# Cross-covariance attention with a mixture of adapters: transposes in 32-bit words of two bf16 channels, and gating weights with A in one operand

## The chip, the cores and the metric

The kernel runs on one core of a Trainium2 chip. The time is device microseconds of one execution. Three runs of the kernel before gave a median of 253.76 us (253.75 to 253.85).

## The reference

There are four batches of N = 6400 rows and C = 256 channels, in float32. Each batch goes through cross-covariance attention, and its result through a mixture of eight adapters of rank 16, of which each row uses two:

```python
qn = q / (np.linalg.norm(q, axis=1, keepdims=True) + 1e-06)
kn = k / (np.linalg.norm(k, axis=1, keepdims=True) + 1e-06)
s = kn.transpose(0, 2, 1) @ qn / tau          # 256 x 256 per batch
a = softmax(s, axis=-1)
x = v @ a                                      # 25600 rows in all
logits = x @ w_gate                            # 8 experts, the best two per row
w = softmax(logits of the best two)
out = x + sum over the two: w * ((x @ A[e]) @ B[e])
```

(`softmax` stands here for the lines of the reference that subtract the maximum, exponentiate and divide.)

## The kernel before, in words

**Layout.** A chunk is 128 rows of one batch, 50 chunks to a batch, 25 pairs of chunks. Partition p of a batch holds 50 neighbouring rows, so that a load of n chunks moves a stretch of n rows into each partition. q, k and v are cast to bf16 by their loads, which GpSimd issues (L212); all but the first piece of q, which SyncE loads as float32. One core does everything.

**First half of a batch: the 256 x 256 matrix.** `gram` (L344) multiplies, for each chunk and each half `ic` of the channels, 128 channels of k (stationary) with all 256 channels of q (moving) into one accumulator `acc` (L350). Beside it the squares of q and k are taken (L323, L326), pairs of chunks added (L335), and summed over the rows by a product with ones (`norm`, L365). `chain0` to `chain6` then make the softmax: roots and reciprocals of the norms, scaling, a product of `ones_f` with a diagonal matrix in float32 (L404) that spreads q's norms over the partitions, and the exponential `ae` (L415).

**From the softmax to the operands of the second half.** `chain4` (L420) transposes `ae` into `aT`: four 128 x 128 transposes of bf16 (L428), whose stationary operand takes every second column, and one copy out of PSUM (L432). `chain5` (L438) multiplies `aT` with `wg_sb`, the gating weights (8 columns, L445), and with `A_sb` (all adapters' A, 128 columns, L447), eight products for a batch, and scales the result into `wa_sb`. `chain6` makes `a_bf`, the softmax itself in bf16.

**Second half: rows of v.** A unit is two pairs, four chunks (or one pair at the end of a group).
- `transposes` (L498): eight 128 x 128 transposes of v in bf16 (L511), then one copy out of PSUM into `vT` on ScalarE or VectorE (L518, L521). `vT` holds `[half of the channels, chunk, row]`.
- `logits` (L530): 8-column products of `vT` with the first 8 columns of `wa_sb` (L539), for a whole group of units; `gating` (L546) makes the two weights of each row from them on VectorE, by a handful of small operations.
- `z_gz` (L634): 128-column products of `vT` with the rest of `wa_sb` (L643), and one VectorE product with the gates (L647) into `gz`, `[chunk, expert and rank]`.
- `gz_t` (L654): a transpose of `gz` for each chunk (L659), and a copy into `gzT` (L664, L667).
- `y_mm` (L671) and `delta` (L681): for each chunk two 256-column products of `vT` with `a_bf` (L676) and one of `gzT` with `ball_sb`, all adapters' B (L685), into one PSUM tile; a copy to `ys` (L695, L698).
- `send` (L708): stores of up to ten pairs, issued by GpSimd for most of the run, by ScalarE and SyncE near the end. The last two, of four pairs and of one, go out through SyncE (L731).

**What sets the order.** There is no scheduler at run time. The main loop (L760) plays through a model of the engines, with a clock for each (`run("pe", 0.1125 * nch)` is the cost that it books for a unit's transposes), and writes each engine's instructions in the order that comes out. The same model picks ScalarE or VectorE for a copy (`quicker`, L527) and the moment at which a load is issued (`load_more`, L179: at most six tiles of q and k and three of v are held). TensorE gets the chain of the next batch first, then logits, then the pairs' stages or the next batch's `gram`, whichever is behind.

Of the kernel before, what the change touches and what calls it, by code (L numbers as in the profile page):

```python
# [8 lines left out]
FP32 = mybir.dt.float32  # L9
BF16 = mybir.dt.bfloat16  # L10
# [6 lines left out]
def kernel(  # L17
# [47 lines left out]
    STAGED = []  # L65
# [159 lines left out]
    for lo, hi in zip([0] + STAGED, STAGED + [P]):  # L225
        nc.sync.dma_start(stage[lo:hi], q_v[0, lo:hi, 0:FIRST, :])
# [32 lines left out]
    wg_sb = const.tile([P, CC, E], BF16)  # L259
    A_sb = const.tile([P, CC, ER], BF16)  # L260
# [9 lines left out]
    def constants():  # L270
        V = nc.vector
        V.tensor_copy(wg_sb.rearrange("p cc e -> p (cc e)"), wst)
# [6 lines left out]
        V.tensor_copy(shift[:, E:E + P].rearrange("p (g j) -> p g j", j=E)[:, :, 0], grp)  # L279
        for e in range(E):  # L280
            V.tensor_scalar(out=a_wide[:, :, e, :], in0=ast, scalar1=own[:, e:e + 1],
                            scalar2=None, op0=OP.mult)

    def constant_a():
        full = ps_t.tile([P, 512], FP32, tag="pt", name="A_ps")
        ap = full.rearrange("p (c k) -> p c k", c=CC)[:, :, 0:ER]
        for j in range(E):
            for cc in range(CC):
                nc.tensor.matmul(
                    ap[:, cc, :], shift[:, E - j:E - j + P],  # L290
                    a_wide[:, CC * j + cc, :, :].rearrange("p e r -> p (e r)"),
                    start=(j == 0 and cc == 0), stop=(j == E - 1), skip_group_check=True)
        nc.vector.tensor_copy(A_sb, ap)
# [126 lines left out]
    def chain4(b):  # L420
        d = st[b]
        ae = d["ae"]
        aT_ps = ps_t.tile([P, 512], FP32, tag="pt", name="aT_ps").bitcast(BF16).rearrange(
            "p (a c i) -> p a c i", a=2, c=CC)[:, 0, :, :]
        aev = ae.rearrange("p ic (m cc) -> p ic cc m", cc=CC)
        for cc in range(CC):
            for ic in range(CC):
                nc.tensor.matmul(aT_ps[:, cc, ic * P:(ic + 1) * P], aev[:, ic, cc, :], ident,  # L428
                                 is_transpose=True, start=(cc == 0 and ic == 0),
                                 stop=(cc == CC - 1 and ic == CC - 1))  # L430
        aT = tmp.tile([P, CC, C], BF16, name="aT")
        nc.vector.tensor_copy(aT, aT_ps)  # L432
        rec = bat.tile([P, CC], FP32, name="rec")
        nc.vector.reciprocal(rec, d["se"])
        d["aT"], d["rec"] = aT, rec
        d["at"] = run("dve", 0.6, run("pe", 0.25, d["at"]))

    def chain5(b):  # L438
# [4 lines left out]
        for ic in range(CC):  # L443
            for cc in range(CC):
                nc.tensor.matmul(wa[:, ic, 0:E], aT[:, cc, ic * P:(ic + 1) * P], wg_sb[:, cc, :],  # L445
                                 start=(cc == 0 and ic == 0), stop=False, skip_group_check=True)
                nc.tensor.matmul(wa[:, ic, E:E + ER], aT[:, cc, ic * P:(ic + 1) * P],  # L447
                                 A_sb[:, cc, :],
                                 start=False, stop=(cc == CC - 1 and ic == CC - 1),
# [48 lines left out]
    def transposes(u):  # L498
# [4 lines left out]
        vT = vt_pool.tile([P, CC, 4, P], BF16, tag="vT", name="vT")[:, :, 0:nch, :]  # L503
        full = ps_t.tile([P, 512], FP32, tag="pt", name="vT_ps")
        pt = full.bitcast(BF16).rearrange("p (c s t) -> p c s t", c=CC, s=4)[:, :, 0:nch, :]
        i = 0
        for sc in range(nch):
            s, o = v_at[2 * p + sc]
            vt = tiles["v"][b, s]
            for ic in range(CC):  # L510
                nc.tensor.matmul(pt[:, ic, sc, :], vt[:, o, ic * P:(ic + 1) * P], ident,  # L511
                                 is_transpose=True, start=(i == 0), stop=(i == 2 * nch - 1))
                i += 1
# [3 lines left out]
        if quicker(0.16 + 0.213 * nch, 0.14 + 0.142 * nch) == "act":  # L517
            nc.scalar.copy(vT, pt)  # L518
# [11 lines left out]
    def logits(gr):  # L530
# [5 lines left out]
        for u in range(gr["u0"], gr["u1"]):  # L536
            for sc in range(2 * units[u]["n"]):
                for ic in range(CC):
                    nc.tensor.matmul(lp[:, i, :], units[u]["vT"][:, ic, sc, :], st[b]["wa"][:, ic, 0:E],  # L539
# [94 lines left out]
    def z_gz(u):  # L634
# [6 lines left out]
        for sc in range(nch):  # L641
            for ic in range(CC):
                nc.tensor.matmul(z[:, sc, :], r["vT"][:, ic, sc, :], st[b]["wa"][:, ic, E:E + ER],  # L643
                                 start=(sc == 0 and ic == 0), stop=(sc == nch - 1 and ic == 1),
                                 skip_group_check=True)
        gz = work.tile([P, 4, ER], BF16, tag="gz", name="gz")[:, 0:nch, :]
        nc.vector.tensor_tensor(  # L647
            out=gz.rearrange("p c (e r) -> p c e r", e=E),
# [5 lines left out]
    def gz_t(u):  # L654
        r = units[u]
        nch = 2 * r["n"]
        gt = r["zg"].bitcast(BF16)[:, 0:512].rearrange("p (s d) -> p s d", s=4)[:, 0:nch, :]
        for sc in range(nch):
            nc.tensor.matmul(gt[:, sc, :], r["gz"][:, sc, :], ident, is_transpose=True,  # L659
                             start=(sc == 0), stop=(sc == nch - 1))  # L660
        gzT = work.tile([P, 4, ER], BF16, tag="gzT", name="gzT")[:, 0:nch, :]
        t_end = run("pe", 0.056 * nch)
        if quicker(0.16 + 0.107 * nch, 0.14 + 0.071 * nch) == "act":
            nc.scalar.copy(gzT, gt)  # L664
            r["gzT_end"] = run("act", 0.16 + 0.107 * nch, t_end)
        else:
            nc.vector.tensor_copy(gzT, gt)  # L667
# [3 lines left out]
    def y_mm(p):  # L671
        r, x = unit_of[p]
        y = ps_y.tile([P, 2, C], FP32, tag="y", name="y_ps")
        for sc in range(2):
            for ic in range(CC):
                nc.tensor.matmul(y[:, sc, :], r["vT"][:, ic, 2 * x + sc, :], st[r["b"]]["a"][:, ic, :],  # L676
# [4 lines left out]
    def delta(p):  # L681
        r, x = unit_of[p]
        gr, y = stores[p], pr[p]["y"]
        for sc in range(2):
            nc.tensor.matmul(y[:, sc, :], r["gzT"][:, 2 * x + sc, :], ball_sb, start=False,  # L685
# [258 lines left out]
```

## Time and profile before

| what | value |
|---|---|
| median of three runs | 253.76 us |
| the profiled execution | 253.88 us |
| its span, from the first to the last instruction | 252.1 us |
| mean granted TensorE clock | 0.945 |
| transposes of v, mean of one (L511) | 219 ns, 400 of them |
| transposes of the gated z, mean of one (L659) | 219 ns, 200 of them |
| copies of vT: VectorE (L521), ScalarE (L518) | 36 of 659 ns, 16 of 1014 ns |
| copies of gzT: VectorE (L667), ScalarE (L664) | 33 of 409 ns, 19 of 577 ns |
| HBM read and written | 78.91 and 26.21 MB |

A group's row in the profile reads: line, engine, operation, output <- input, shape, count | busy us, mean ns of one | idle time of the engine before it, and what ended most of that. PE is TensorE's products, PEld its loads of stationary operands, which run beside the products. Products are pipelined: the mean of one is from its start to its modelled end, and the next one starts long before that, so the spacing of products is read from the chain of waits, where a row gives the start, the length and the count of a run of products. A row of a window gives, after the stretch and its length, the busy us of PE, PEld, DVE, ACT and POOL with their counts, the granted clock, the DMA share and GB/s. Loads that cast to bf16 are counted in GB/s by what they write, which is half of what they read.

### The profile page before, as it was taken

What the parts mean: (1) busy time and instruction counts of PE and PEld (TensorE: products, weight loads), DVE (VectorE), ACT (ScalarE), POOL (GpSimd) and SP (SyncE); (2) the same over time, 40 slices, a digit from 0 to 9 for tenths busy, and PEclk for the clock granted to TensorE, in tenths of its full rate; (3) what the DMA queues carried; (4) which work ended last, traced back from release to release, by engine and by line L of the source; (5) the groups of instructions that cost most, each with busy time, mean ns of one, the idle gap of its engine ahead of it and who ended that gap; (6) DMA issues with size and microseconds to landing.
All of it is one profiled execution on the core that took longest, in us unless ns stands there. A gap on an engine that the chain in (4) does not pass through costs nothing.

```text
span 252.1 us, 6727 instructions
## 1 busy us (share of the span) xinstructions
PE 205.5 (82%) x2870; PEld 183.5 (73%) x2870; DVE 165.2 (66%) x420; ACT 167.1 (66%) x256; POOL 31.1 (12%) x63
## 2 busy tenths in 40 slices
PE   0457087576499999999999899898999989999950
PEld 0344076465478999999989788797998878999940
DVE  1541646784539688887957798769687677687510
ACT  2654065873739779899565698966798757586640
POOL 8111003004001200030401101030020000010000
PEclk9997659999859999999999999999999999999995
DMA  7999999999999999999999999999999999999995
GB/s 218 214 214 212 238 220 213 212 217 213 216 214 218 216 213 215 214 216 215 216 409 230 214 217 216 251 414 388 221 217 218 256 376 305 432 432 408 424 423 217
DMA packets 8902, 66.76 MB, mean 265 GB/s; under 512 B 984, under 2 KB 1128, under 8 KB 5416
## 3 DMA queue, kind: packets, MB, share of 16 engines
q0 software_dynamic: 7872, 60.04, 94.2%
q10 hardware_dynamic: 432, 3.74, 3.5%
q1 hardware_dynamic: 568, 2.56, 2.7%
q8 instruction: 22, 0.36, 0.5%
q14 instruction: 8, 0.07, 0.1%
HBM read 78.91 MB, written 26.21 MB: 417 GB/s over the span
## 4 chain that ended last, share of the span: by engine, by line
DMA 42%; PE 39%; DVE 6%; issue 5%; ACT 3%; POOL 2%; DVEq 0%; POOLq 0%; ACTq 0%
DMA vt<-in_v_dram 14%; PE y_ps L676 10%; DMA kt<-in_k_dram 10%; DMA qt<-in_q_dram 10%; DMA bst<-in_moe_B_dram 8%; PE acc L350 8%; PE y_ps L685 5%; PE zg L643 4%; PE vT_ps L511 4%; PE zg L659 2%; PE lp L539 2%; DVE s L335 2%; ACT sq L326 2%; PE nrm L365 1%; ACT ys L698 1%
## 5 line engine op out<-in xcount | busy, mean ns | idle before, releaser
L698 ACT COPY ys<-y_ps 128x512 f32<-128x512 f32 x92 | 52.1, 586 | 15.6 <-PE y_ps L685 14.3
L350 PE MATMUL acc<-qt,kt 128*128 128x256 bf16 x400 | 56.7, 293 | 5.4 <-DMA kt<-in_k_dram 5.4
L676 PE MATMUL y_ps<-a_bf,vT 128*128 128x256 bf16 x400 | 59.2, 272 | 1.6 <-ACT ys L698 1.5
L326 ACT ACTIVATE sq<-qt 128x1024 bf16<-128x1024 bf16 (+1 forms) x42 | 40.7, 1013 | 14.6 <-DVE s L335 11.0
L326 ACT ACTIVATE sq<-kt 128x1024 bf16<-128x1024 bf16 (+1 forms) x43 | 42.1, 1013 | 11.1 <-DMA kt<-in_k_dram 5.5
L350 PEld LDWEIGHTS <-kt 128*128 128x128 bf16 x400 | 39.5, 104 | 12.7 <-DMA kt<-in_k_dram 6.0
L335 DVE TENSOR_TENSOR s<-sq 128x512 bf16<-128x512 bf16 x104 | 38.6, 408 | 5.7 <-ACT sq L326 3.3
L647 DVE TENSOR_TENSOR gz<-zg,e 128x512 bf16<-128x512 f32 (+1 forms) x52 | 33.9, 666 | 11.9 <-PE zg L643 11.7
L676 PEld LDWEIGHTS <-vT 128*128 128x128 bf16 x400 | 36.2, 98 | 5.5 <-issue 2.3
L365 PE MATMUL nrm<-ones_bf,s 128*128 128x1 bf16 x398 | 21.1, 165 | 23.3 <-DVE s L335 21.3
L365 PEld LDWEIGHTS <-s 128*128 128x128 bf16 x398 | 18.4, 97 | 27.0 <-DVE s L335 24.5
L685 PE MATMUL y_ps<-ball_sb,gzT 128*128 128x256 bf16 x200 | 36.2, 272 | 0.0
L511 PE MATMUL vT_ps<-ident,vt 128*128 128x128 bf16 x400 | 30.3, 219 | 4.1 <-DMA vt<-in_v_dram 3.0
L521 DVE COPY vT<-vT_ps 128x1024 bf16<-128x1024 bf16 (+1 forms) x36 | 23.6, 659 | 13.0 <-PE vT_ps L511 12.5
L643 PE MATMUL zg<-wa_sb,vT 128*128 128x128 bf16 x400 | 30.0, 221 | 0.0
L511 PEld LDWEIGHTS <-vt 128*128 128x128 bf16 x400 | 24.9, 98 | 5.9 <-DMA vt<-in_v_dram 3.6
L643 PEld LDWEIGHTS <-vT 128*128 128x128 bf16 x400 | 25.6, 99 | 0.7
L518 ACT COPY vT<-vT_ps 128x1024 bf16<-128x1024 bf16 x16 | 16.1, 1014 | 11.4 <-PE vT_ps L511 11.4
L212 POOL DMA_DIRECT2D qt<-in_q_dram x16 | 8.6, 538 | 95.3 <-ACT sq L326 49.3
L659 PE MATMUL zg<-ident,gz 128*128 128x128 bf16 x200 | 19.3, 219 | 0.5 <-DVE gz L647 0.3
L667 DVE COPY gzT<-zg 128x512 bf16<-128x512 bf16 (+1 forms) x33 | 13.3, 409 | 9.2 <-PE zg L659 9.0
L664 ACT COPY gzT<-zg 128x512 bf16<-128x512 bf16 (+1 forms) x19 | 11.0, 577 | 12.4 <-PE zg L659 11.8
(71 smaller groups left out, 176.1 us busy)
## 6 DMA issues: line engine op xcount, KB each, us to landing
out_dram<-ys POOLq DMA_DIRECT2D x8, 2560.0 KB, 35.7
qt<-in_q_dram POOLq DMA_DIRECT2D x12, 768.0 KB, 22.1
kt<-in_k_dram POOLq DMA_DIRECT2D x12, 768.0 KB, 25.0
vt<-in_v_dram POOLq DMA_DIRECT2D x8, 1024.0 KB, 29.0
vt<-in_v_dram POOLq DMA_DIRECT2D x4, 1152.0 KB, 28.5
kt<-in_k_dram POOLq DMA_DIRECT2D x4, 896.0 KB, 21.3
qt<-in_q_dram POOLq DMA_DIRECT2D x3, 896.0 KB, 20.6
out_dram<-ys ACTq DMA_DIRECT2D x2, 1280.0 KB, 10.0
```

The source lines that it names most:

```text
L326: nc.scalar.activation(sq, x, ACT.Square)
L335: nc.vector.tensor_tensor(out=s2, in0=sq[:, 0:n, :], in1=sq[:, n:2 * n, :], op=OP.add)
L350: nc.tensor.matmul(acc[b][:, ic, :], tk[:, o, ic * P:(ic + 1) * P], tq[:, o, :], start=(c == 0 and ic == 0), stop=(c == NC - 1), skip_grou ...
L365: nc.tensor.matmul(nrm[b][:, j:j + 1], s2[:, x, ic * P:(ic + 1) * P], ones_bf[:, 0:1], start=(i == 0 and x == 0 and ic == 0), stop=(i >= l ...
L511: nc.tensor.matmul(pt[:, ic, sc, :], vt[:, o, ic * P:(ic + 1) * P], ident, is_transpose=True, start=(i == 0), stop=(i == 2 * nch - 1))
L521: nc.vector.tensor_copy(vT, pt)
L643: nc.tensor.matmul(z[:, sc, :], r["vT"][:, ic, sc, :], st[b]["wa"][:, ic, E:E + ER], start=(sc == 0 and ic == 0), stop=(sc == nch - 1 and ...
L647: nc.vector.tensor_tensor(out=gz.rearrange("p c (e r) -> p c e r", e=E), in0=z.rearrange("p c (e r) -> p c e r", e=E), in1=gr["gate"][:, r ...
L659: nc.tensor.matmul(gt[:, sc, :], r["gz"][:, sc, :], ident, is_transpose=True, start=(sc == 0), stop=(sc == nch - 1))
L676: nc.tensor.matmul(y[:, sc, :], r["vT"][:, ic, 2 * x + sc, :], st[r["b"]]["a"][:, ic, :], start=(sc == 0 and ic == 0), stop=False, skip_gr ...
L685: nc.tensor.matmul(y[:, sc, :], r["gzT"][:, 2 * x + sc, :], ball_sb, start=False, stop=(sc == 1), skip_group_check=True)
L698: nc.scalar.copy(dst, y)
```

## The change

Two neighbouring channels of bf16 are taken as one 32-bit word. A transpose of 128 words for each of 128 rows then moves all 256 channels at once: partition m of the result holds channels 2m and 2m+1 of a row beside each other. So v's transposes go from eight to four for a unit, those of the softmax from four to two for a batch. For the gated z the two chunks of a pair are put beside each other: the VectorE product with the gates (L647) writes `gz` with the chunk as its last index, and the transposes go from four to two for a unit. The identity that is multiplied with is `ident_f`, in float32, which the kernel made already.

The halves of the channels are now the even and the odd ones, no longer the first and the second 128. For this, k's channels are taken in that order, by a step of two, as stationary operand of `gram` and of k's norms; q's stay. All products that have `vT`, `aT` or `gzT` as the stationary operand read it at a step of two. The copies out of PSUM take the 32-bit result as twice as many bf16 elements, so they move what they moved.

`wg_sb` and `A_sb` become one tile `wga`, so that `chain5` has four products of 136 columns for a batch in place of four of 8 and four of 128. In all 324 products go: 200 + 100 + 8 transposes and 16 of `chain5`. In the instruction stream a 32-bit transpose stands as one product without a separate load of weights.

The costs that the planner books are unchanged. On VectorE, ScalarE, GpSimd and SyncE the instructions stand in the same order as before, and on TensorE the stages too.

```diff
@@ constants
-    wg_sb = const.tile([P, CC, E], BF16)
-    A_sb = const.tile([P, CC, ER], BF16)
+    wga = const.tile([P, CC, E + ER], BF16)
...
-        V.tensor_copy(wg_sb.rearrange("p cc e -> p (cc e)"), wst)
+        V.tensor_copy(wga[:, :, 0:E], wst.rearrange("p (cc e) -> p cc e", cc=CC))
...
-        nc.vector.tensor_copy(A_sb, ap)
+        nc.vector.tensor_copy(wga[:, :, E:E + ER], ap)
@@ gram, norm
-                acc[b][:, ic, :], tk[:, o, ic * P:(ic + 1) * P], tq[:, o, :],
+                acc[b][:, ic, :], tk[:, o, :].rearrange("p (m i) -> p i m", i=CC)[:, ic, :], tq[:, o, :],
...
+                y = s2[:, x, :].rearrange("p (m i) -> p i m", i=CC)[:, ic, :] if w else s2[:, x, ic * P:(ic + 1) * P]
-                    nrm[b][:, j:j + 1], s2[:, x, ic * P:(ic + 1) * P], ones_bf[:, 0:1],
+                    nrm[b][:, j:j + 1], y, ones_bf[:, 0:1],
@@ chain4
-        aev = ae.rearrange("p ic (m cc) -> p ic cc m", cc=CC)
-        for cc in range(CC):
-            for ic in range(CC):
-                nc.tensor.matmul(aT_ps[:, cc, ic * P:(ic + 1) * P], aev[:, ic, cc, :], ident,
-                                 is_transpose=True, start=(cc == 0 and ic == 0),
-                                 stop=(cc == CC - 1 and ic == CC - 1))
-        aT = tmp.tile([P, CC, C], BF16, name="aT")
-        nc.vector.tensor_copy(aT, aT_ps)
+        aT_ps = ps_t.tile([P, 512], FP32, tag="pt", name="aT_ps")[:, 0:CC * P]
+        for ic in range(CC):
+            nc.tensor.matmul(aT_ps[:, ic * P:(ic + 1) * P], ae[:, ic, :].bitcast(FP32), ident_f,
+                             is_transpose=True, start=(ic == 0), stop=(ic == CC - 1))
+        aT = tmp.tile([P, C, CC], BF16, name="aT")
+        nc.vector.tensor_copy(aT.rearrange("p i cc -> p (i cc)"), aT_ps.bitcast(BF16))
@@ chain5
-                nc.tensor.matmul(wa[:, ic, 0:E], aT[:, cc, ic * P:(ic + 1) * P], wg_sb[:, cc, :],
-                                 start=(cc == 0 and ic == 0), stop=False, skip_group_check=True)
-                nc.tensor.matmul(wa[:, ic, E:E + ER], aT[:, cc, ic * P:(ic + 1) * P],
-                                 A_sb[:, cc, :],
-                                 start=False, stop=(cc == CC - 1 and ic == CC - 1),
+                nc.tensor.matmul(wa[:, ic, :], aT[:, ic * P:(ic + 1) * P, cc], wga[:, cc, :],
+                                 start=(cc == 0 and ic == 0), stop=(cc == CC - 1 and ic == CC - 1),
@@ transposes
-            for ic in range(CC):
-                nc.tensor.matmul(pt[:, ic, sc, :], vt[:, o, ic * P:(ic + 1) * P], ident,
-                                 is_transpose=True, start=(i == 0), stop=(i == 2 * nch - 1))
-                i += 1
+            nc.tensor.matmul(pt[:, sc * P:(sc + 1) * P], vt[:, o, :].bitcast(FP32), ident_f,
+                             is_transpose=True, start=(i == 0), stop=(i == nch - 1))
+            i += 1
...
-            nc.vector.tensor_copy(vT, pt)
+            nc.vector.tensor_copy(vT.rearrange("p s t i -> p (s t i)"), pt.bitcast(BF16))
@@ logits; z_gz and y_mm read vT in the same way
-                    nc.tensor.matmul(lp[:, i, :], units[u]["vT"][:, ic, sc, :], st[b]["wa"][:, ic, 0:E],
+                    nc.tensor.matmul(lp[:, i, :], units[u]["vT"][:, sc, :, ic], st[b]["wa"][:, ic, 0:E],
@@ z_gz
-        gz = work.tile([P, 4, ER], BF16, tag="gz", name="gz")[:, 0:nch, :]
+        gz = work.tile([P, ER * 4], BF16, tag="gz", name="gz")[:, 0:ER * nch].rearrange(
+            "p (d c) -> p d c", c=nch)
         nc.vector.tensor_tensor(
-            out=gz.rearrange("p c (e r) -> p c e r", e=E),
+            out=gz.rearrange("p (e r) c -> p c e r", e=E),
@@ gz_t
-        for sc in range(nch):
-            nc.tensor.matmul(gt[:, sc, :], r["gz"][:, sc, :], ident, is_transpose=True,
-                             start=(sc == 0), stop=(sc == nch - 1))
+        words = r["gz"].rearrange("p d c -> p (d c)").bitcast(FP32).rearrange("p (d x) -> p x d", x=r["n"])
+        for x in range(r["n"]):
+            nc.tensor.matmul(gt[:, x * P:(x + 1) * P], words[:, x, :], ident_f, is_transpose=True,
+                             start=(x == 0), stop=(x == r["n"] - 1))
@@ delta
-            nc.tensor.matmul(y[:, sc, :], r["gzT"][:, 2 * x + sc, :], ball_sb, start=False,
+            nc.tensor.matmul(y[:, sc, :], r["gzT"][:, x, :, sc], ball_sb, start=False,
```

More of the change, by code (lines that the diff above doesn't have):

```diff
@@ L224 @@
     stage = y_pool.tile([P, 2 * YG, C], FP32, tag="ys", name="stage")[:, 0:FIRST, :]
-    for lo, hi in zip([0] + STAGED, STAGED + [P]):
-        nc.sync.dma_start(stage[lo:hi], q_v[0, lo:hi, 0:FIRST, :])
+    nc.sync.dma_start(stage, q_v[0, :, 0:FIRST, :])
     wst = const.tile([P, CC * E], FP32)
@@ L502, in transposes @@
         nch = 2 * r["n"]
-        vT = vt_pool.tile([P, CC, 4, P], BF16, tag="vT", name="vT")[:, :, 0:nch, :]
-        full = ps_t.tile([P, 512], FP32, tag="pt", name="vT_ps")
-        pt = full.bitcast(BF16).rearrange("p (c s t) -> p c s t", c=CC, s=4)[:, :, 0:nch, :]
+        vT = vt_pool.tile([P, 4, P, CC], BF16, tag="vT", name="vT")[:, 0:nch, :, :]
+        pt = ps_t.tile([P, 512], FP32, tag="pt", name="vT_ps")[:, 0:nch * P]
         i = 0
@@ L517, in transposes @@
         if quicker(0.16 + 0.213 * nch, 0.14 + 0.142 * nch) == "act":
-            nc.scalar.copy(vT, pt)
+            nc.scalar.copy(vT.rearrange("p s t i -> p (s t i)"), pt.bitcast(BF16))
             end = run("act", 0.16 + 0.213 * nch, t_end)
         else:
-            nc.vector.tensor_copy(vT, pt)
+            nc.vector.tensor_copy(vT.rearrange("p s t i -> p (s t i)"), pt.bitcast(BF16))
             end = run("dve", 0.14 + 0.142 * nch, t_end)
@@ L675, in y_mm @@
             for ic in range(CC):
-                nc.tensor.matmul(y[:, sc, :], r["vT"][:, ic, 2 * x + sc, :], st[r["b"]]["a"][:, ic, :],
+                nc.tensor.matmul(y[:, sc, :], r["vT"][:, 2 * x + sc, :, ic], st[r["b"]]["a"][:, ic, :],
                                  start=(sc == 0 and ic == 0), stop=False, skip_group_check=True)
```

14 lines of the change are left out of this document (6 added, 8 removed).

## The prediction, made before the changed kernel had run

> **What bounds the kernel now.** I read the page's busy shares and slices first, then the window views for the DMA share, then the chain of waits backwards from the end.
>
> ```profile
> PE 205.5 (82%) x2870; PEld 183.5 (73%) x2870; DVE 165.2 (66%) x420; ACT 167.1 (66%) x256; POOL 31.1 (12%) x63
> DMA  7999999999999999999999999999999999999995
> 3.00:247.00 244.00, 205.47 (x2870) 183.51 (x2870) 164.92 (x417) 165.84 (x255) 29.15 (x57) 0.95 1.03 269
> ```
>
> The last two figures of a window row are DMA share and GB/s. From 3 to 247 us the DMA share is 1.03, so nearly all of the span is covered by transfers, and the change removes no byte. PE looks busy for 82%, but ends of products are modelled, so I look at what PE does in the last stretch.
>
> ```profile
> 168.43 35.88 DMA vt<-in_v_dram
> 204.35 0.40 PE vT_ps L511 x4
> ...
> 207.18 0.45 PE vT_ps L511 x8
> ...
> 208.38 0.22 PE zg L659 x4
> 208.61 0.44 PE y_ps L676 x4
> ...
> 209.72 0.98 PE lp L539 x40
> ...
> 242.57 0.29 PE y_ps L685 x2
> 242.88 0.58 ACT ys L698
> ```
>
> These are rows of the chain: start, length, what. They give start-to-start costs that the mean durations hide: eight 16-bit transposes of v take 0.45 us (56 ns each), four of the gated z 0.22 (55 ns), a 256-column product 0.44/4 = 110 ns, an 8-column logit product 0.98/40 = 24.5 ns. From 204.35, when a load of v lands, to 242.9 the chain is PE alone. So the end of the computation is a sum of PE work, while everything earlier waits on transfers. Behind it comes a drain:
>
> ```profile
> 243.49 1.26 SPq L731 DMA_DIRECT2D out_dram<-ys  x1
> out_dram<-ys SPq DMA_DIRECT2D x1, 1024.0 KB, 8.0
> out_dram<-ys SPq DMA_DIRECT2D x1, 256.0 KB, 7.7
> 246.00:247.00 1.00, 0.00 (x0) 0.00 (x0) 0.00 (x0) 0.00 (x0) 0.00 (x0) 0.50 1.00 419
> 247.00:248.00 1.00, 0.00 (x0) 0.00 (x0) 0.00 (x0) 0.00 (x0) 0.00 (x0) 0.50 0.79 330
> 248.00:249.00 1.00, 0.00 (x0) 0.00 (x0) 0.00 (x0) 0.00 (x0) 0.00 (x0) 0.50 0.72 297
> 249.00:250.00 1.00, 0.00 (x0) 0.00 (x0) 0.00 (x0) 0.00 (x0) 0.00 (x0) 0.50 0.48 193
> 250.00:251.00 1.00, 0.00 (x0) 0.00 (x0) 0.00 (x0) 0.00 (x0) 0.00 (x0) 0.50 0.16 61
> ```
>
> The last store is issued at 243.49 and lands 7.7 us later; the transfers stay full until 247 and then thin out. The unused share from 247 to 251 is 0.21+0.28+0.52+0.84 = 1.85 us. That is about all that an earlier end of the computation can win; a later end costs most of itself once the backlog (3.5 us from 243.5 to 247) is eaten, and part of itself before.
>
> **The change part by part.** The order of instructions on DVE, ACT, POOL and SP is the same in both kernels, and so is PE's order of stages, because the planner's costs were left as they are. So only durations differ. Terms are counted in the PE stretch at the end:
>
> ```profile
> L643 PE MATMUL zg<-wa_sb,vT 128*128 128x128 bf16 x112 | 8.5, 219 | 0.0
> L659 PE MATMUL zg<-ident,gz 128*128 128x128 bf16 x64 | 6.3, 219 | 0.0
> L511 PE MATMUL vT_ps<-ident,vt 128*128 128x128 bf16 x64 | 5.1, 219 | 1.0 <-DMA vt<-in_v_dram 1.0
> L539 PE MATMUL lp<-wa_sb,vT 128*128 128x8 bf16 x100 | 2.9, 166 | 0.0
> L447 PE MATMUL wa_ps<-A_sb,aT 128*128 128x128 bf16 x4 | 0.5, 216 | 0.0
> ```
>
> *Transposes.* Removed: 64 + 64 of 16 bits, 128 x 56 ns = 7.2 us. Added: 64 of 32 bits. No 32-bit transpose is in the trace; the only 32-bit product is the broadcast of L404:
>
> ```profile
> L404 PEld LDWEIGHTS nrm<-dg,ones_f x8: 187/190/192, 44.9 to 201.2; 128*128 128x128 f32 x8
> L404 PE MATMUL nrm<-dg,ones_f x8: 379/380/455, 45.0 to 201.4; 128*128 128x256 f32 x8
> 87.17 0.30 PEld L404 LDWEIGHTS nrm<-dg,ones_f 128*128 128x128 f32 x2
> 158.23 0.60 PE L404 MATMUL nrm<-dg,ones_f 128*128 128x256 f32 x2
> ```
>
> Each batch issues it once, and the trace has eight: the chip makes two passes of a 32-bit product. Two weight loads span 0.30 us and one lasts 190 ns, so they start 110 ns apart. Two products span 0.60 us at 380 ns each, so they start 220 ns apart: 256 columns at twice the 110 ns of 16 bits, and 110 ns for 128 columns. The ends for one 32-bit transpose are therefore 56 ns (no dearer than a 16-bit one) and 220 ns (two passes at 110). I take one pass: a transpose moves its data and adds nothing, so no second pass has a sum to complete; and 110 ns for it, the row's spacing of weight loads. That is 64 x 110 = 7.0 us for 7.2: nothing gained by the pace itself. What is left open is the product. If it too takes 110 ns, a group of four costs 0.44 us for 0.45. If it takes 56, the load of the next stage slips under it and a group costs 3 x 110 + 56 = 386 ns for 448, a gated-z pair 110 + 56 = 166 for 224: with 8 groups of v and 16 pairs, 8 x 62 + 16 x 58 = 1.4 us at the end. I take the middle, 0.7 us.
>
> The Trainium skill (TensorE: Matmul & The Clock Gate, section "Weight-path perf modes — Fast Weight Load (FWL) and DoubleRow") says that the fast load of weights is given to 128 weights of a type other than FP32, which speaks against this change; 190 ns, beside the 96 to 98 of the 16-bit rows below, agrees. Its section "Terms" says that a transpose mode makes FP32 four times faster; by it the product would take 56 ns and the sum would be 1.4 us. No row here shows that mode.
>
> *Strided operands.* v's, the softmax's and k's stationary operands are now read at every second 16-bit element, the gated z's words at every second 32-bit one. The trace has one strided 16-bit load, L428, beside a packed one:
>
> ```profile
> L428 PEld LDWEIGHTS <-ae x16: 96/98/98, 48.0 to 206.0; 128*128 128x128 bf16 x16
> L539 PEld LDWEIGHTS <-vT x400: 95/96/98, 64.2 to 227.0; 128*128 128x128 bf16 x134
> ```
>
> 98 against 96 ns: I take no cost. But L428's loads stand 56 ns apart, so a hidden cost up to 56 ns shows nowhere; it would bite only where products are shorter, the logits and the norms: up to 56 - 24.5 = 31 ns on 100 logit products, 3.1 us at the end. A strided load could not be faster than the packed one, so there is no gain below zero.
>
> *DVE and ACT.* The copies of vT, gzT and aT move the same counts. The gate product writes at a step of four elements:
>
> ```profile
> L647 DVE TENSOR_TENSOR gz<-zg,e 128x512 bf16<-128x512 f32 (+1 forms) x52 | 33.9, 666 | 11.9 <-PE zg L643 11.7
> L279 DVE CAST shift<-grp 128x16 bf16<-128x16 f32 x1 | 0.2, 205 | 0.0
> L272 DVE CAST wg_sb<-wst 128x16 bf16<-128x16 f32 x1 | 0.2, 174 | 7.3 <-DMA wst<-in_moe_w_gate_dram 7.3
> ```
>
> L279 writes 16 elements at a step of eight, L272 packed: 31 ns more, 2 ns an element, which for 512 would be 1.0 us a call. 666 ns for 512 elements is already an element at a time, so I take 0, with 1.0 us as the upper end; a gain is excluded since no element is saved. DVE is busy 66%, which hides a small part of such a cost.
>
> *Gating weights and A in one operand.* Per batch 4 products of 8 columns go (24.5 ns each, 0.1 us) and 4 grow by 8 columns; the transposes of the softmax go from 4 to 2 (4 x 56 = 224 to 2 x 110 = 220 ns). One batch stands in the end stretch (L447 x4 above): 0.1 us. The two copies into it are made once, ahead of the first batch's softmax, as before.
>
> *Before 204 us* PE gains or loses likewise, but the loads there land by the transfers ahead of them (35.88 us from issue), so I count 0.
>
> **Sum.** The computation ends 0.7 + 0.1 = 0.8 us earlier. The transfers are full till 247, so of this about half comes through (1.85 us unused, spread over the whole drain): 0.4 us. The profiled run took 253.88 us for a span of 252.1 (1.8 around it), 0.12 above the median of 253.76. 253.76 - 0.4 = 253.4 us.
>
> **Rivals.**
> 1. *Even better pace* (56 ns for a 32-bit transpose): 64 x 54 = 3.5 us off the end stretch, but the drain allows at most 1.85: 252.3. Against it: the 110 ns between 32-bit loads.
> 2. *Nothing arrives*: product and load at 110 ns, the order and the transfers unchanged: 253.7. For it: the DMA row at 9 throughout.
> 3. *Slower, the price of one 32-bit transpose.* The point is 112 ns, two of 16 bits. It decides in two stretches, at the end and from 80 to 204 us:
>
> ```profile
> 80.00:204.30 124.30, 119.48 (x1762) 109.41 (x1759) 97.22 (x239) 98.03 (x155) 14.03 (x26) 1.00 1.03 253
> 204.30:242.90 38.60, 38.13 (x544) 35.14 (x544) 25.49 (x67) 25.72 (x49) 1.24 (x2) 1.00 1.01 397
> L511 PE MATMUL vT_ps<-ident,vt 128*128 128x128 bf16 x272 | 20.7, 219 | 0.5 <-DMA vt<-in_v_dram 0.5
> L659 PE MATMUL zg<-ident,gz 128*128 128x128 bf16 x128 | 12.2, 219 | 0.5 <-DVE gz L647 0.3
> ```
>
> If the next load can't start under the running product (110 + 56 = 166 ns), the end stretch grows by 64 x 54 = 3.5 us, of which the drain absorbs one; the 400 transposes of the middle become 200 and cost 10.8 us more, against 124.3 - 119.5 = 4.8 us in which PE is not busy there: 253.8 + 2.5 + 6.0 = 262. With two passes (220 ns) it is 64 x 108 = 6.9 us at the end and 21.6 in the middle: 253.8 + 6.4 + 16.8 = 277. For it: L404's two passes; against it: no sum to complete.
> 4. *Slower, strided loads* in the 24.5 ns stages: 3.1 us more at the end, the drain absorbs a third: 255.8. Against it: 98 beside 96 ns.
> 5. *Slower, the strided write* at 1.0 us more a call (a call for four transposes): the middle's DVE has 97.2 + 32 us of work in 124.3, the end's 25.5 + 16 in 38.6, so DVE becomes the bound: 253.8 + 4.9 + 2.9 = 262 at least.
>
> **How the numbers follow.** Runs differ by 0.1 us, so 0.2% (0.5 us) is about what a measurement tells from no change. Forecast: 45%, its own range 252.9 to 253.8, about half of it below 253.25. Rival 1: 8%. Rival 2: 18%. Rival 3: 15% (two thirds at 262, one at 277). Rival 4: 10%. Rival 5: 4%. Faster: 23 + 8 + 2 = 33%. Same: 22 + 16 = 38%. Slower: 15 + 10 + 4 = 29%. The range leaves out rivals 3 and 5 (19%) and keeps 1 and 4, with 4's full 3.1 us: 252.2 to 257.0.
>
> **What would show it.** One 32-bit weight load and one product for each transpose (200, 100 and 8 of them); the chain's group of four v transposes at 0.39 to 0.44 us; logit products still 0.98 for 40; L647 still near 666 ns; the last store issued near 242.7; DMA share full till 246 or 247. I am wrong if the 32-bit rows come twice, if a group takes over 0.5 us, or if the last store moves by over 1.5 us.

## The result, and the profile after

The changed kernel takes 265.75 us (264.8 to 266.76) against 253.75 (253.72 to 253.85) for the one before, measured side by side: a ratio of 1.047 [1.043, 1.051], 12.0 us slower. The profiled execution took 264.8 us for a span of 263.0, so the same 1.8 us lie around the span and all the loss is inside it (263.0 - 252.1 = 10.9 us in the profiled pair).

From the page of the kernel after: busy time by engine, the DMA row of the 40 slices, and the shares of the chain that ended last.

```profile
PE 218.8 (83%) x2546; PEld 186.0 (71%) x2546; DVE 189.2 (72%) x420; ACT 167.7 (64%) x256; POOL 31.0 (12%) x63
DMA  7999999999999999999999999999999999818685
PE 44%; DVE 27%; DMA 18%; issue 4%; ACT 3%; POOL 2%; DVEq 0%; POOLq 0%
```

TensorE has its 324 products fewer, as announced. VectorE runs the same 420 instructions and is busy 24.0 us longer (189.2 - 165.2; its instructions overlap a little, and their durations add up to more). The DMA row has holes near the end, where before it stood at 9 up to the last slice. And the chain has changed hands; the same line of the page before reads:

```profile
DMA 42%; PE 39%; DVE 6%; issue 5%; ACT 3%; POOL 2%; DVEq 0%; POOLq 0%; ACTq 0%
```

VectorE's part rose from 6% to 27%, that of the transfers fell from 42% to 18%. Which instruction it is, the groups of the kernel after tell, each shape by itself (line, what, count | busy us, mean ns of one | idle time before it, what ended it):

```profile
L638 DVE TENSOR_TENSOR gz<-zg,e 128x512 bf16<-128x512 f32 x48 | 60.8, 1316 | 8.9 <-PE zg L633 8.7
L638 DVE TENSOR_TENSOR gz<-zg,e 128x256 bf16<-128x256 f32 x4 | 1.8, 444 | 0.2 <-PE zg L633 0.2
L501 PEld LDWEIGHTS vT_ps<-ident_f,vt 128*128 128x128 f32 x200 | 22.5, 141 | 2.6 <-ACT vT L508 1.2 <-DVE vT L511 0.9
L651 PEld LDWEIGHTS zg<-ident_f,gz 128*128 128x128 f32 x100 | 15.5, 203 | 16.2 <-DVE gz L638 15.2 <-DVE m L555 0.5 <-DVE ed L586 0.3
```

The gate product L638 (L647 before) has nearly doubled for whole units of four chunks, from 687 ns (the row of before is below, with the first experiment) to 1316. The half units, which hold two chunks and so write at a step of two elements and not four, stayed near their old price: 444 ns. The 32-bit transposes stand once each in the trace, a load and a product, 200 and 100 of them, so there is no second pass. Their loads are longer than the 16-bit ones, and longest for the gated z, whose words lie two words apart: 203 ns.

The waits of the kernel after (engine, waited for: us in all, times, longest), and below them those of before at the same places:

```profile
PEld zg L651 <- DVE gz L638: 15.2, 35, 1.0
PE zg L651 <- DVE gz L638: 5.8, 19, 0.9
...
POOL vt L211 <- PE vT_ps L501: 32.6, 6, 16.4
```

```profile
PEld L659 <- DVE gz L647: 0.9, 3, 0.4
...
POOL vt L212 <- PE vT_ps L511: 25.9, 6, 11.1
```

The two rows of the gated z show the same waits, once on the loads and once on the products: the 5.8 us lie inside the 15.2 and aren't added to them. So TensorE, whose order is fixed, now stands before the transposes of the gated z for 15.2 us, 0.9 before. GpSimd, which issues the loads, waits 6.7 us longer until v's transposes give a buffer back. The chain of the kernel after shows it as a beat that comes again and again (start, length, what):

```profile
235.32 0.44 PE vT_ps L501 x4
...
252.43 0.46 PE zg L633 x8
252.91 1.32 DVE gz L638
254.27 0.50 PE zg L651 x2
...
257.34 0.59 ACT ys L691
```

TensorE makes z, VectorE multiplies for 1.32 us, TensorE transposes. The four transposes of v take 0.44 us, 110 ns each, as forecast. The last copy ends at 257.93, 14.5 us later than before (243.46).

Where those 14.5 us gathered can be read from two other lines: the row of a line gives the start of its first and last instruction. First the kernel after, then the one before.

```profile
L347 PE MATMUL acc<-qt,kt x400: 269/273/421, 9.9 to 206.7; 128*128 128x256 bf16 x134
L211 POOL DMA_DIRECT2D vt<-in_v_dram x12: 531/536/551, 19.3 to 193.8; - x12
```

```profile
L350 PE MATMUL acc<-qt,kt x400: 269/273/421, 10.1 to 195.5; 128*128 128x256 bf16 x134
L212 POOL DMA_DIRECT2D vt<-in_v_dram x12: 528/533/558, 19.5 to 183.5; - x12
```

By the last product of the last `gram` 11.2 us have been lost, and the last load of v is issued 10.3 us later. So most of the delay lies ahead of the end stretch. The transfers do not fall behind with it. Here is that last load of v in the DMA issues of its stretch (size, us from issue to landing): first of the kernel after, 193.5 to 194.5 us, then of the one before, 183 to 184.5 us.

```profile
vt<-in_v_dram POOLq DMA_DIRECT2D x1, 1024.0 KB, 19.8
```

```profile
vt<-in_v_dram POOLq DMA_DIRECT2D x1, 1024.0 KB, 31.4
```

Issued at 193.8 it lands at 213.6; before, issued at 183.5, it landed at 214.9. What it lost in being issued it no longer spent behind other transfers. Two windows of the kernel after show the same:

```profile
80.00:204.30 124.30, 116.28 (x1450) 102.55 (x1450) 104.13 (x221) 90.04 (x139) 14.05 (x26) 1.00 1.03 254
230.00:240.00 10.00, 9.68 (x138) 8.84 (x139) 8.73 (x21) 6.40 (x12) 0.71 (x1) 1.00 0.49 203
```

Up to 204.3 us the transfers are as full as before (1.03, 254 GB/s for 253), and the DMA row stands at 9 for 34 of its 40 slices, to about 224 us. The holes come behind that: the loads are all in, only stores are left, and they wait for rows that TensorE, over 10 us late, has yet to make. The drain gives a little of the delay back:

```profile
out_dram<-ys SPq DMA_DIRECT2D x1, 256.0 KB, 4.2
```

With the transfers no longer behind, the last store lands 4.2 us after its issue in place of 7.7: 14.5 - 3.5 = 11.0, the 10.9 us of the spans.

### The profile page after: what moved, and what is told of

Same layout as the page of the kernel before. It is cut to its first block, busy times and chain, and to the rows that moved or that the text cites. A ratio compares the mean times of both kernels' runs of the same rounds, so it can differ in the third digit from the quotient of the medians.

```text
span 263.0 us, 6082 instructions
## 1 busy us (share of the span) xinstructions
PE 218.8 (83%) x2546; PEld 186.0 (71%) x2546; DVE 189.2 (72%) x420; ACT 167.7 (64%) x256; POOL 31.0 (12%) x63
## 4 chain that ended last, share of the span: by engine, by line
PE 44%; DVE 27%; DMA 18%; issue 4%; ACT 3%; POOL 2%; DVEq 0%; POOLq 0%
DVE gz L638 17%; PE y_ps L669 10%; PE acc L347 10%; DMA kt<-in_k_dram 9%; DMA bst<-in_moe_B_dram 8%; PE y_ps L678 6%; PE zg L651 6%; PE vT_ps L501 4%; PE zg L633 3%; PE lp L529 2%; DVE s L332 2%; PE nrm L363 2%; ACT sq L323 2%; DVE tk L404 1%; ACT ys L691 1%
## 5 line engine op out<-in xcount | busy, mean ns | idle before, releaser
L638 DVE TENSOR_TENSOR gz<-zg,e 128x512 bf16<-128x512 f32 (+1 forms) x52 | 62.6, 1249 | 9.0 <-PE zg L633 8.8
L347 PE MATMUL acc<-qt,kt 128*128 128x256 bf16 x400 | 61.1, 309 | 3.2 <-DMA kt<-in_k_dram 3.2
L347 PEld LDWEIGHTS <-kt 128*128 128x128 bf16 x400 | 42.4, 111 | 12.2 <-DMA kt<-in_k_dram 3.4
L669 PEld LDWEIGHTS <-vT 128*128 128x128 bf16 x400 | 38.1, 98 | 5.2 <-issue 1.6
L501 PE MATMUL vT_ps<-ident_f,vt 128*128 128x128 f32 x200 | 30.0, 275 | 1.1 <-ACT vT L508 0.7
L651 PE MATMUL zg<-ident_f,gz 128*128 128x128 f32 x100 | 24.1, 322 | 7.3 <-DVE gz L638 5.8
L651 PEld LDWEIGHTS zg<-ident_f,gz 128*128 128x128 f32 x100 | 15.5, 203 | 16.2 <-DVE gz L638 15.2
L633 PEld LDWEIGHTS <-vT 128*128 128x128 bf16 x400 | 25.9, 98 | 0.7
L501 PEld LDWEIGHTS vT_ps<-ident_f,vt 128*128 128x128 f32 x200 | 22.5, 141 | 2.6 <-ACT vT L508 1.2
L508 ACT COPY vT<-vT_ps 128x1024 bf16<-128x1024 bf16 x16 | 16.1, 1014 | 11.6 <-PE vT_ps L501 11.6
```

Of the source, the lines that this page charges most:

```text
L347: nc.tensor.matmul(acc[b][:, ic, :], tk[:, o, :].rearrange("p (m i) -> p i m", i=CC)[:, ic, :], tq[:, o, :], start=(c == 0 and ic == 0), s ...
L501: nc.tensor.matmul(pt[:, sc * P:(sc + 1) * P], vt[:, o, :].bitcast(FP32), ident_f, is_transpose=True, start=(i == 0), stop=(i == nch - 1))
L633: nc.tensor.matmul(z[:, sc, :], r["vT"][:, sc, :, ic], st[b]["wa"][:, ic, E:E + ER], start=(sc == 0 and ic == 0), stop=(sc == nch - 1 and ...
L638: nc.vector.tensor_tensor(out=gz.rearrange("p (e r) c -> p c e r", e=E), in0=z.rearrange("p c (e r) -> p c e r", e=E), in1=gr["gate"][:, r ...
L651: nc.tensor.matmul(gt[:, x * P:(x + 1) * P], words[:, x, :], ident_f, is_transpose=True, start=(x == 0), stop=(x == r["n"] - 1))
L669: nc.tensor.matmul(y[:, sc, :], r["vT"][:, 2 * x + sc, :, ic], st[r["b"]]["a"][:, ic, :], start=(sc == 0 and ic == 0), stop=False, skip_gr ...
```

## The experiments

**The theories.** Mine after the result: the write at a step of four elements makes the gate product slow, and TensorE waits for it. The rival: the price lies in TensorE itself, in the 32-bit transposes or the operands at a step. Every ratio is to the kernel before, timed on the same chip. Line numbers are those of each kernel.

**e1: the changed kernel with the gated z as before** (packed write, four 16-bit transposes; all else changed).

```diff
-            out=gz.rearrange("p (e r) c -> p c e r", e=E),
+            out=gz.rearrange("p c (e r) -> p c e r", e=E),
...
+            nc.tensor.matmul(gt[:, sc, :], r["gz"][:, sc, :], ident, is_transpose=True,
```

> The changed kernel with the gated z alone as before (written packed, 16-bit transposes); v, the softmax, k's order and the joined operand stay changed. Theory W (the gate product's write at a step of four elements carries the loss: 1316 ns for 690): 253.75 us, within 0.3. Theory L (the 32-bit weight load at a step of two words carries it: a pair of transposes in 0.50 us for 0.22): also 253.75, since that goes too. Theory V (v's 32-bit transposes, the operands read at a step of two): above 254.5.

**e2: the reverse, the kernel before with the gated z's part alone.**

```diff
-            out=gz.rearrange("p c (e r) -> p c e r", e=E),
+            out=gz.rearrange("p (e r) c -> p c e r", e=E),
...
+            nc.tensor.matmul(gt[:, x * P:(x + 1) * P], words[:, x, :], ident_f, is_transpose=True,
```

> The kernel before with the gated z alone changed (strided write, two 32-bit transposes a unit). W and L: 265 to 266 us, as the whole change. V: under 255.

**e3: the kernel before with the write of the gate product alone at a step of four; the 16-bit transposes read the tile packed.**

```diff
-            out=gz.rearrange("p c (e r) -> p c e r", e=E),
+            out=gz.rearrange("p (e r) c -> p c e r", e=E),
...
-            nc.tensor.matmul(gt[:, sc, :], r["gz"][:, sc, :], ident, is_transpose=True,
+            nc.tensor.matmul(gt[:, sc, :], r["gz"].rearrange("p d c -> p (d c)")[:, sc * ER:(sc + 1) * ER], ident,
```

> The kernel before with the gated z written at a step of four elements, but its 16-bit transposes read the tile packed, so the gated z that comes out has its elements in the wrong places. W: the gate product 1.3 us for 0.69, four transposes still in 0.22 us, 262 to 265 us in all. L: the gate product may be longer, but the time stays under 255.

**e4: the kernel before with the packed write, and two 32-bit transposes that read words two words apart.**

```diff
+        words = r["gz"].rearrange("p c d -> p (c d)").bitcast(FP32).rearrange("p (d x) -> p x d", x=r["n"])
+            nc.tensor.matmul(gt[:, x * P:(x + 1) * P], words[:, x, :], ident_f, is_transpose=True,
```

> The kernel before with the gated z written packed and transposed in two 32-bit products a unit whose words are read at a step of two, so the words hold the wrong neighbours. L: a pair of transposes in 0.50 us, 262 us or more. W: the gate product at 0.69 us; the end stretch has 16 pairs, 16 x 0.28 = 4.5 us more of PE, of which the drain absorbs a part: 255 to 257.5 us.

Measured: e1 253.69 us, 0.9998 [0.9989, 1.0008]; e2 265.54, 1.045 [1.041, 1.049]; e3 262.54, 1.035 [1.033, 1.036]; e4 253.60, 0.9997 [0.9988, 1.0006]. The gated z's part carries all of the loss, and the rest of the change nothing. The gate product in the groups of the kernel before, and below it in those of e3:

```profile
L647 DVE TENSOR_TENSOR gz<-zg,e 128x512 bf16<-128x512 f32 x48 | 32.2, 687 | 11.7 <-PE zg L643 11.5
```

```profile
L648 DVE TENSOR_TENSOR gz<-zg,e 128x512 bf16<-128x512 f32 x48 | 60.5, 1310 | 11.2 <-PE zg L643 11.1
```

e3's waits on the loads, and a row of its chain:

```profile
PEld L660 <- DVE gz L648: 15.3, 34, 1.0
```

```profile
229.19 0.40 PE zg L660 x4
```

Two rows of e4's chain, whose gate product took 687 ns as before:

```profile
204.44 0.24 PE zg L660 x2
215.93 0.29 PE zg L660 x2
```

The write alone has the whole price of the instruction and the same 15 us of waiting, and it costs 8.9 us. The 32-bit load of words two apart costs nothing by itself: a pair goes through in 0.24 to 0.29 us, since the loads run beside the products ahead. When TensorE has just waited nothing runs ahead, and a pair then takes 0.50 us (after) where four 16-bit ones take 0.40 (e3). That is 0.1 us on each of some 35 waits, 3.5 us as an estimate, beside the 3.0 us by which e2 is slower than e3. So the rival seems to hold in a small part: the load costs where the slow write has already made TensorE wait. This is worked out from the rows; no run shows it by itself.

e1 also tells what the faster parts are worth. The last copy of its chain stands at 241.50 and takes 0.59 us. A row of its DMA issues:

```profile
out_dram<-ys SPq DMA_DIRECT2D x1, 256.0 KB, 8.9
```

Its computation ends at 242.09, 1.4 us before that of the kernel before, and its last store takes 1.2 us longer to land (8.9 for 7.7).

**e5: a step of two in place of four**: the tile as `[pair, channel, chunk of the pair]`, so that the words are packed too. **e6: the layout of the change, but written in the order of addresses**, so that the steps are on the side that reads z and the gates. **e7: e5, with ScalarE's copies of vT and gzT as 32-bit words.**

```diff
# e5
+        gz = work.tile([P, 2, ER, 2], BF16, tag="gz", name="gz")[:, 0:r["n"], :, :]
+            out=gz.rearrange("p x (e r) s -> p x s e r", e=E),
+        words = r["gz"].rearrange("p x d s -> p x (d s)").bitcast(FP32)
# e6
+            out=gz.rearrange("p (e r) c -> p e r c", e=E),
+            in0=z.rearrange("p c (e r) -> p e r c", e=E),
# e7
+            nc.scalar.copy(vT.rearrange("p s t i -> p (s t i)").bitcast(FP32), pt)
+            nc.scalar.copy(dst.bitcast(FP32), gt)
```

> The changed kernel with the two chunks of a pair beside each other and the pairs one after the other, so that the gate product writes at a step of two elements (4 bytes) and the words are read packed. Theory W with a price that depends on the step: the half units of the changed kernel already write at a step of two and take 444 ns for 420, so about 0.74 us a call instead of 1.32, a pair of transposes in 0.22 us, and 253.7 us within 0.3. If every step costs the same: still 1.3 us a call and 262 or more.

> The changed kernel with the same layout of the gated z, but the gate product goes through it in the order of its addresses: it writes packed and reads z out of PSUM and the gates at a step. If writes to addresses 8 bytes apart are what costs: about 0.7 us a call and 253.7 to 255. If any step in this product costs, on whichever side: 1.2 us or more a call and 262 or more.

> The step-of-two kernel with ScalarE's copies of vT and gzT made as 32-bit words (512 and 256 elements for 1024 and 512): from 1014 to about 590 ns and from 577 to about 370 ns a copy. If the transfers set the end, as the first two kernels without the strided write say (compute ended 1.4 us earlier, the time did not move): 253.7 us within 0.3. If the path through ScalarE matters at the end: 252.5 to 253.2.

Measured: e5 253.57 us, 0.9996 [0.9987, 1.0005]; e6 256.13, 1.0089 [1.0073, 1.0106]; e7 253.56, 0.9994 [0.9985, 1.0002]. Groups of e5, then of e6:

```profile
L637 DVE TENSOR_TENSOR gz<-zg,e 128x512 bf16<-128x512 f32 x48 | 34.3, 735 | 8.8 <-PE zg L633 8.6
L650 PEld LDWEIGHTS zg<-ident_f,gz 128*128 128x128 f32 x100 | 11.8, 140 | 1.5 <-DVE gz L637 1.0
```

```profile
L640 DVE TENSOR_TENSOR gz<-zg,e 128x512 bf16<-128x512 f32 x48 | 49.0, 1041 | 10.9 <-PE zg L633 10.8
L640 DVE TENSOR_TENSOR gz<-zg,e 128x256 bf16<-128x256 f32 x4 | 1.7, 420 | 0.2 <-PE zg L633 0.2
```

At a step of two the loss is gone. e6 came out between the two expectations: reading at a step costs too, for four chunks (1041 ns) and not for two (420 ns, as packed). Why it does so for four alone, no run tells. A group of e7:

```profile
L508 ACT COPY vT<-vT_ps 128x512 f32<-128x512 f32 x16 | 9.4, 586 | 12.0 <-PE vT_ps L501 12.0
```

A copy of vT on ScalarE took 586 ns, where it took 1014 before, and the time did not move.

**e8: the kernel before with the gate product written at steps of 1, 2, 3, 4 and 6 elements in turn,** into one shared buffer, 16-bit transposes reading at the same step. The shared buffer puts waits of its own into it, so its time (278.09 us, one run) says nothing; its instructions do.

```diff
+        step = [1, 2, 3, 4, 6][u % 5]
+        gz = big[:, 0:nch * ER * step].rearrange("p (c e r k) -> p c e r k", c=nch, e=E, k=step)[:, :, :, :, 0]
```

> The kernel before with the gated z written, unit by unit in turn, at steps of 1, 2, 3, 4 and 6 elements into one buffer, and its 16-bit transposes reading at the same step; each step has a line of its own. For the mean of one product: if the price begins beyond 4 bytes, 0.69, 0.74, then 1.3 us for 3, 4 and 6; if it grows with the step, 0.69, 0.74, 1.0, 1.3, 1.9. The whole time says nothing, since one buffer makes the units wait for each other.

The groups of e8: L652 writes at a step of 1, L654 of 2, L656 of 3, L658 of 4, L660 of 6; L680 is the 16-bit load at a step of 6.

```profile
L652 DVE TENSOR_TENSOR big<-zg,e 128x512 bf16<-128x512 f32 x10 | 6.9, 688 | 7.0 <-PE zg L644 6.8
L654 DVE TENSOR_TENSOR big<-zg,e 128x512 bf16<-128x512 f32 x10 | 7.3, 732 | 1.2 <-PE zg L644 0.8
L656 DVE TENSOR_TENSOR big<-zg,e 128x512 bf16<-128x512 f32 x9 | 9.1, 1012 | 0.9 <-PE zg L644 0.8
L658 DVE TENSOR_TENSOR big<-zg,e 128x512 bf16<-128x512 f32 x9 | 11.7, 1296 | 3.2 <-PE zg L644 2.8
L660 DVE TENSOR_TENSOR big<-zg,e 128x512 bf16<-128x512 f32 x10 | 18.7, 1869 | 1.8 <-PE zg L644 1.5
L680 PEld LDWEIGHTS <-big 128*128 128x128 bf16 x40 | 3.2, 134 | 8.5 <-DVE big L652 3.4 <-DVE big L660 2.9 <-DVE m L566 2.1
```

The write is nearly free up to a step of two (44 ns), then costs 280 to 287 ns for each further element of step, 0.55 to 0.56 ns for one element written. The stationary load pays far less: 98 ns at a step of 1 and 2, 134 at 6. The Trainium skill (SBUF — State Buffer, section "Door 1: The DMA port swizzle (why `[64,N]` ≈ `[32,N]`)") says that on-chip memory has lines of 16 bytes and that two accesses to a line suffice for the full pace. By that rule the step of four bf16 elements, 8 bytes, would be free and the change would have cost nothing here. The rows differ: the price begins between 4 and 6 bytes and grows evenly with the step up to the 12 bytes measured. The measurement decides.

**e9: the kernel before without the 200 products of the gated z with B, so that the adapters' part is missing from the output.** It takes TensorE work away at the end, to see what an earlier end is worth.

```diff
-        for sc in range(2):
-            nc.tensor.matmul(y[:, sc, :], r["gzT"][:, 2 * x + sc, :], ball_sb, start=False,
-                             stop=(sc == 1), skip_group_check=True)
```

> The kernel before without the 200 products of the gated z with B, so that the adapters' part is missing from the output: 64 x 110 ns = 7 us less PE work in the end stretch, 22 us less in all. If the transfers set the end: 253.4 to 253.8 us. If an earlier end of the computation still comes through in part, as the prediction had it (half, up to 1.85 us): 252.0 to 252.5.

Measured: 253.77 us, 1.0004 [0.9994, 1.0013]. The end of its chain, and a row of its DMA issues:

```profile
237.20 0.59 ACT ys L695
```

```profile
out_dram<-ys SPq DMA_DIRECT2D x1, 256.0 KB, 13.0
```

The computation ends 5.7 us earlier (237.79 for 243.46) and the last store lands 13.0 us after its issue in place of 7.7: the transfers give nothing of it back.

**e10: the changed kernel, with the planner told what the gate product now costs** (`0.16 + 0.29 * nch` us in place of `0.15 + 0.133 * nch`), so that it puts other work between.

```diff
-        r["gz_end"] = run("dve", 0.15 + 0.133 * nch, run("pe", 0.1125 * nch), gr["gate_end"])
+        r["gz_end"] = run("dve", 0.16 + 0.29 * nch, run("pe", 0.1125 * nch), gr["gate_end"])
```

> The changed kernel with the planner told the gate product's real cost (0.16 + 0.29 us a chunk, so 1.32 for four, in place of 0.68); nothing else differs. If the loss is PE's waiting in an order that was made for a shorter product: much of it comes back, 255 to 260 us. If VectorE's added work itself is the bound: 264 to 266, as without it.

Measured: 264.41 us, 1.040 [1.035, 1.045], an interval that overlaps that of the unaltered change. Waits of e10, and below them one of the unaltered change:

```profile
PEld zg L651 <- DVE gz L638: 6.3, 10, 2.9
PE acc L347 <- DMA kt<-in_k_dram: 7.1, 5, 2.2
```

```profile
PE acc L347 <- DMA kt<-in_k_dram: 3.2, 3, 1.3
```

The wait for `gz` fell from 15.2 to 6.3 us, and the time did not follow: the new order moves loads and copies as well, and the waits for k's loads grew from 3.2 to 7.1 us. So a better-informed order didn't win the time back. The time fell into the range that had been set down for "VectorE's added work itself is the bound". The waits for `gz` are therefore not shown to be the whole path from the slow write to the lost time; how much is the order and how much VectorE's load, this run does not part.

**e11: the kernel before with its packed gate product issued twice. e12: with a second, packed product over one of the four chunks alone.** Both keep every layout, and give VectorE more time to spend. They ask whether the strided write does harm other than by its duration, and where the cost begins.

```diff
# e11
+        for _ in range(2):
# e12
+        nc.vector.tensor_tensor(
+            out=gz.rearrange("p c (e r) -> p c e r", e=E)[:, 0:1],
```

> The kernel before with the packed gate product issued twice in a row into the same tile, so that VectorE spends 2 x 0.69 = 1.37 us a unit on it, all else as before. If the strided write harms by VectorE's time alone: about what the strided write alone gave (1.31 us a unit, 262.5 us), so 262.5 to 264. If the strided write also disturbs other engines or transfers: clearly less, under 261.

> The kernel before with the packed gate product followed by a second one over the first of the four chunks alone, into the same place: about 0.69 + 0.25 = 1.0 us a unit, between the 0.69 of before and the 1.31 of the strided write. Theory of a cover (the order leaves PE other work for a time after z; only what is longer than that is waited for, but then in full, as from 1.31 to 1.43 us a unit with 52 units the time grew by 7.9 us): under 255.0. Theory of a bound (each us of VectorE's work costs its share): on the line from 253.7 to 262.5, so 257 to 259.

Measured: e11 270.39 us, 1.065 [1.063, 1.067]; e12 253.93, 1.0007 [0.9998, 1.0017]. A group of e11, and its waits on the loads:

```profile
L648 DVE TENSOR_TENSOR gz<-zg,e 128x512 bf16<-128x512 f32 x96 | 65.0, 688 | 12.4 <-PE zg L643 10.5
```

```profile
PEld L660 <- DVE gz L648: 22.2, 39, 1.2
```

The same of e12, and the end of its chain:

```profile
L651 DVE TENSOR_TENSOR gz<-zg,e 128x128 bf16<-128x128 f32 x52 | 15.2, 292 | 1.8
```

```profile
PEld L663 <- DVE gz L651: 6.1, 19, 0.8
```

```profile
245.41 0.59 ACT ys L702
```

VectorE's time alone suffices to make such a loss; nothing else about the strided write is needed. e11 missed its expectation on the high side, though a unit of it takes 2 x 688 ns, 1.38 us (the 1.43 in e12's expectation is too much). In order of what was added to the gate product (all calls together, the four half units with them):

| run | gate product, us more in all | computation ends, us | time, us |
|---|---|---|---|
| before | 0 (33.9 in all) | 243.46 | 253.75 |
| e12 | 15.2 | 246.00 | 253.93 |
| e6 (with the rest of the change) | 16.8 | 249.07 | 256.13 |
| e3 | 28.4 | 256.20 | 262.54 |
| e11 | 34.5 | 264.35 | 270.39 |

The first 0.3 us for a unit are free. TensorE does wait 6.1 us for them, but the computation ends only 2.5 us later, and the drain swallows that. In every row below the first the time grows by 2.4 to 4.3 us less than the end of the computation moves, which is what the drain takes up. Beyond the first 0.3 us the cost is steep, and from e3 to e11 more than one for one (6.1 us of VectorE for 7.9 us of time). Why it is as steep as that is open.

None of these versions beats both kernels: e1, e5 and e7 beat the changed one and can't be told from the one before.

## Why the prediction was wrong

**The step that failed** is in "DVE and ACT": "666 ns for 512 elements is already an element at a time, so I take 0, with 1.0 us as the upper end". It measured +0.63 us for a whole unit (1316 against 687 ns), and this write alone costs 8.9 us (e3). The two nearest rows, 205 ns at a step of eight and 174 packed, gave 2 ns an element; e8's 0.56 ns for each element of step beyond two gives 3.4 ns at a step of eight, and 1.1 at four. So the small rows pointed at a real price, and I set it aside by an argument about pace which no row supported. Their end, 1.0 us, was the nearer one.

**Rival 5**, the strided write, was the case that came true, with "262 at least" and 4%. That its 262 lies near the 265.75 measured is in part luck: its price of 1.0 us stands against 0.63, and its mechanism, "DVE becomes the bound", is not what the rows show. With the measured price its own sum for the middle, 97.2 + 32 x 0.63 = 117.4 us of work, fits into the 124.3, and in the window of the kernel after VectorE is busy for 104.13 of these 124.30 us. It hands its delay to TensorE, whose written order and drain cover some 0.3 us more for a unit (e12) and not 0.63; e10 leaves open how much VectorE's load adds to that. "DVE is busy 66%, which hides a small part of such a cost" was right in kind; what hides is the room in the order, not the busy share.

**"Before 204 us", "so I count 0"**, did not hold either: 11.2 of the 14.5 us gathered by the end of the last `gram`. Its premise was right, the loads land by the transfers ahead of them (213.6 us for 214.9). But TensorE waited 3.0 us for v's loads before and has no such wait after: once it is late enough nothing holds it up there, and its delay stays.

**"About half comes through"** was wrong too. Nothing comes through: 1.4 us in e1, 1.6 in e5 (its last copy ends at 241.84) and 5.7 in e9 all went into the landing of the last store. The 1.85 us that I read as unused share in the drain could not be won, so without the slow write the time is that of rival 2, 253.7, as e1 (253.69) and e5 (253.57) measured. The other half of that reading held: the backlog of 3.5 us takes up a later end, 14.5 us for 10.9 in the spans.

**What held.** The kernel before is bound by its transfers. A 32-bit transpose goes once, at 110 ns: 0.44 us for four, and no second pass, so rival 3 is out. "Strided operands" are free for 16 bits: e1 has all of v's, the softmax's and k's. The logits still take 0.98 us for 40, in e1 and below it before:

```profile
217.93 0.98 PE lp L529 x40
241.50 0.59 ACT ys L688
```

```profile
219.28 0.98 PE lp L539 x40
242.88 0.58 ACT ys L698
```

**The 0.7 + 0.1 us expected at the end** are not what e1 gained. It is 1.35 us ahead at these logits and 1.38 at the last copy, so nearly all of its lead was won earlier; and a group of v's transposes takes 0.44 us in e1's chain too, for 0.45. Of the two ends in "Transposes" it was the one without a gain that came true. The Trainium skill (TensorE: Matmul & The Clock Gate, section "Terms") says that transpose mode makes FP32 four times faster. The rows show twice: a 32-bit product like L404's costs 220 ns for 128 columns (two passes of 220 for 256), a 32-bit transpose 110. Whether the product or its load sets these 110 ns, no run tells apart.

**What the prediction left out** is what a new wait uncovers. A load of 203 ns is hidden as long as TensorE has products ahead of it, and not behind a wait (by the estimate above; e2 less e3: 3.0 us). I had priced the strided loads beside short products only.

## What to carry to other kernels

A layout that makes one engine's operand wide can make another engine's write slow: look for the instruction that has to write the new order, and give it a price from the nearest strided row, even a small one, rather than from an argument. Choose the interleaving with the smallest step: two bf16 elements were nearly free, four nearly doubled the instruction. And in a kernel whose order is written out, ask for a lengthened instruction not how busy its engine is, but how long the next engine can do without it; where transfers set the end, work that is saved gains nothing, and work that is added costs only once it outlasts that cover.

## What the runs showed that was not expected

- A product on VectorE from float32 in PSUM to bf16 takes 688 ns for 512 columns packed, 732 at a step of two, and then 280 to 287 ns more for each further element of step (1869 ns at six).
- Reading at a step instead cost 1041 ns for four chunks and nothing for two (420 ns).
- A ScalarE copy of 2048 bytes a partition out of PSUM took 586 ns as 512 words of 32 bits, and 1014 as 1024 of 16.
- 5.7 us less computation at the end of a transfer-bound kernel moved its time by 0.0 us, and 2.5 us more by 0.2.
